# A token MLP's first product in layer one: ten of fourteen weight tiles taken as five pairs by seven half products, with two smaller edits elsewhere

## The chip, the cores and the metric

The kernel runs on one core of one Trainium2 chip. The metric is the device time of one execution in microseconds (us), as the median of three runs. A core has a matrix engine (TensorE, PE in the profile, with its weight loads as PEld), VectorE (DVE), ScalarE (ACT), GpSimd (POOL) and SyncE (SP), which issues the DMA transfers. Each engine works through its own list of instructions in order and waits on semaphores for the others.

## The reference, cut to what matters

```python
# x: (1, 2048 tokens, 640 channels); F = 1728 hidden
def _A_ref(x, w_r, w_i):
    X = rfft2(x);  X = X * (w_r + 1j * w_i)
    return irfft2(X, s=(S, D))

def _B_ref(x, w1, b1, w2, b2):
    h = _layernorm(x)                          # over channels
    u = gelu(einsum("bsd,sf->bdf", h, w1) + b1)  # over tokens
    return (einsum("bdf,fs->bds", u, w2) + b2).transpose(0, 2, 1)

x = x + _A_ref(_layernorm(x), A_w_r, A_w_i)    # layer 1, spectral
x = x + _B_ref(_layernorm(x), B_w1, B_b1, B_w2, B_b2)   # layer 1, MLP
x = x + _A_ref(_layernorm(x), A_w_r, A_w_i)    # layer 2, spectral
x = x + _B_ref(_layernorm(x), B_w1, B_b1, B_w2, B_b2)   # layer 2, MLP
```

## The kernel before, in words

All four stages run as matrix products on TensorE. Each factor of a product is split into a high and a low half-precision part, and a product is three matmuls (`mm3`): high weights by high input, high by low, low by high. One matmul has 128 x 128 weights and 320 columns; the 640 channels are two halves of 320 columns. The 2048 tokens are 16 token tiles (`NJ`), the 1728 hidden rows 14 hidden tiles (`NFT`), of which the last is half full. Nearly every instruction is recorded through the helper `call` at L58, so that in the profile the names of the tiles tell instructions apart, not lines.

**Layer one's MLP** is the function `b1st` (L1131). At its start there are 16 normalised token tiles `hf` (single precision) with their high parts `hh`. VectorE makes the low parts `hl` = `hf` - `hh`, 16 subtractions of 640 elements a row, in one go, while TensorE works on what needs only `hh`: `both_high` gives the high products of hidden tiles 0 and 1. Then the loop over the hidden tiles (L1212) runs: for tiles 0 and 1 the 32 matmuls each that need `hl` (`rest`, L1193), for tiles 2 to 12 all 96 matmuls (`both`: 16 token tiles by two halves by three), for tile 13 64. Tile 2's weights can be split only when its scale is known: TensorE sums the squares that ScalarE scanned, VectorE makes the scale from it in a chain of six small instructions (`scale1`, L291; `qt`, `qi`, `s`, `c` in the trace), ScalarE rounds the raw weights to the high part `wh`, VectorE makes the low part `wl`. After each hidden tile ScalarE and VectorE form its gelu (L1250 to L1256) into `uf`. `scale_u` and `usplit` (L1181) split that into `uh` and `ul`, on VectorE. The second product (L1290) takes the 14 hidden tiles in order as inputs for the 16 token tiles, adds the result to x and prepares the next spectral stage; after the last token tile a short chain, `a0_tail` (L603), prepares the last input while TensorE runs `warm` matmuls whose result isn't used.

**Layer two's MLP** (`b2nd`, L1366) already takes its second product in pairs of tiles by seven half products.

The work in these stages stands in the order of the code (`pin` is true) or is left to the framework's scheduler (`pin` is false). The spectral stages are ordered by a planner (`Plan`) from costs and due times in `add(...)` calls.

## Time and profile before

| | |
|---|---|
| median of three runs | 1010.33 us (1010.2 to 1010.74) |
| profiled execution, whole time | 1010.17 us |
| profiled execution, span of the trace | 1008.4 us |
| mean granted TensorE clock | 0.997 |
| busy: TensorE / VectorE / ScalarE / GpSimd | 976.7 / 710.3 / 592.2 / 251.6 us |
| first stage ends, layer one's spectral stage goes on | about 50 us |
| layer one's MLP starts / tile 2 starts / second product starts / ends | 168.2 / 195.7 / 349.0 / 542.7 us |

A row of the profile's timeline gives the start, the time taken by the whole group, the engine, the operation, what it writes `<-` what it reads, the sizes and, behind an x, how many instructions it groups; in brackets the idle time before it and what ended it. The view of windows gives each engine's busy time in a stretch of the span and in brackets the instructions; PEclk is the granted clock of TensorE as a share of the full one.

### The profile page before, as it was taken

What the parts mean: (1) busy time and instruction counts of PE and PEld (TensorE: products, weight loads), DVE (VectorE), ACT (ScalarE), POOL (GpSimd) and SP (SyncE); (2) the same over time, 40 slices, a digit from 0 to 9 for tenths busy, and PEclk for the clock granted to TensorE, in tenths of its full rate; (3) what the DMA queues carried; (4) which work ended last, traced back from release to release, by engine and by line L of the source; (5) the groups of instructions that cost most, each with busy time, mean ns of one, the idle gap of its engine ahead of it and who ended that gap; (6) DMA issues with size and microseconds to landing.
All of it is one profiled execution on the core that took longest, in us unless ns stands there. A gap on an engine that the chain in (4) does not pass through costs nothing. (4 is left out here: it accounts for less than half of the span.)

```text
span 1008.4 us, 22169 instructions
## 1 busy us (share of the span) xinstructions
PE 976.7 (97%) x8981; PEld 718.1 (71%) x8981; DVE 710.3 (70%) x1382; ACT 592.2 (59%) x926; POOL 251.6 (25%) x409
## 2 busy tenths in 40 slices
PE   5899999999999999999998999999999999999998
PEld 4678666777777777777777886667777777777776
DVE  7989678743336777777765896886644755988885
ACT  6978699564444565555542777964644545444531
POOL 7759786000000011111121796840000000000000
PEclk8999999999999999999999999999999999999999
DMA  8774275532222453443325532846222322545411
GB/s 318 252 220 111 80 226 159 163 94 76 84 85 73 141 192 133 140 138 126 106 83 174 161 117 77 236 151 209 85 84 85 95 88 80 163 152 188 145 45 53
DMA packets 53862, 135.75 MB, mean 135 GB/s; under 512 B 6376, under 2 KB 11392, under 8 KB 53760
## 3 DMA queue, kind: packets, MB, share of 16 engines
q1 hardware_dynamic: 53760, 134.35, 41.1%
q8 instruction: 70, 1.15, 0.5%
q14 instruction: 32, 0.26, 0.1%
HBM read 111.25 MB, written 23.07 MB: 133 GB/s over the span
## 5 line engine op out<-in xcount | busy, mean ns | idle before, releaser
L58 PEld LDWEIGHTS <-wh 128*128 128x128 f16 x2992 | 289.9, 98 | 114.1 <-issue 3.3
L58 PEld LDWEIGHTS <-wl 128*128 128x128 f16 x1616 | 158.0, 98 | 61.6
L58 PE MATMUL ps<-hh,wh 128*128 128x320 f16 x896 | 186.5, 299 | 1.6 <-ACT hh L58 1.6
L58 PE MATMUL ps<-hl,wh 128*128 128x320 f16 x896 | 184.7, 299 | 0.0
L58 PE MATMUL ps<-hh,wl 128*128 128x320 f16 x832 | 171.4, 299 | 0.0
L58 DVE SCALAR_TENSOR_TENSOR wl<-raw,s,wh 128x1024 f16<-128x1024 f32 (+2 forms) x88 | 110.5, 1273 | 46.8 <-ACT wh L58 46.7
L58 ACT ACTIVATE wh<-raw,s 128x1024 f16<-128x1024 f32 (+2 forms) x92 | 94.7, 1049 | 65.5 <-PE ps L58 58.9
L58 PE MATMUL ps<-uh,wl 128*128 128x320 f16 x448 | 133.1, 299 | 0.0
L58 PE MATMUL ps<-ul,wh 128*128 128x320 f16 x448 | 133.0, 299 | 0.0
L58 PE MATMUL ps<-uh,wh 128*128 128x320 f16 x416 | 124.3, 299 | 0.0
L58 ACT ACTIVATE junk<-raw 128x896 bf16<-128x896 f32 (+1 forms) x60 | 59.7, 995 | 44.1 <-DMA raw<-w 43.5
L58 PE MATMUL ps<-u,wo 128*128 128x320 f16 x504 | 69.9, 299 | 0.0
L58 DVE TENSOR_TENSOR xt<-xt,ps 128x320 f32<-128x320 f32 (+1 forms) x96 | 45.0, 490 | 30.6 <-ACT ec L58 20.3
L58 POOL TENSOR_TENSOR r<-v,mh 128x1 f32<-128x1 f32 (+1 forms) x56 | 33.6, 600 | 125.6 <-DVE nm L58 112.6
L58 PEld LDWEIGHTS <-wo 128*128 128x128 f16 x504 | 49.3, 98 | 19.1
L58 DVE BATCH_NORM_STATS2 st<-xt 128x6 f32<-128x320 f32 x128 | 56.2, 480 | 3.3 <-DMA xt<-x 2.7
L58 PE MATMUL ps<-tDi,yh 128*128 128x322 f16 x240 | 50.2, 299 | 0.0
L58 DVE TENSOR_SCALAR qt<-ps 128x1 f32<-128x1 f32 x14 | 2.1, 156 | 67.4 <-PE ps L58 67.4
L58 PE MATMUL ps<-u,wh 128*128 128x320 f16 x336 | 48.4, 299 | 0.0
L58 PE MATMUL ps<-u,wl 128*128 128x320 f16 x336 | 48.2, 299 | 0.0
L58 POOL MEMSET uh<- 64x640 f16 x1 | 0.8, 776 | 184.1 <-DVE ul L58 184.1
L58 PE MATMUL ps<-tm,F 128*128 128x128 f32 (+1 forms) x256 | 30.5, 317 | 15.0 <-ACT tm L58 11.5
(177 smaller groups left out, 1879.5 us busy)
## 6 DMA issues: line engine op xcount, KB each, us to landing
raw<-w SPq DMA_DIRECT2D x56, 512.0 KB, 3.6
xt<-x SPq DMA_DIRECT2D x80, 320.0 KB, 3.9
x<-xt SPq DMA_DIRECT2D x48, 320.0 KB, 2.5
raw<-w SPq DMA_DIRECT2D x32, 448.0 KB, 3.3
raw<-w2z SPq DMA_DIRECT2D x32, 448.0 KB, 3.4
w<-w SPq DMA_DIRECT2D x44, 321.0 KB, 3.6
out<-xt SPq DMA_DIRECT2D x15, 320.0 KB
stk<-rest SPq DMA_DIRECT2D x36, 64.0 KB, 2.7
```

Of the source, the lines that this page charges most:

```text
L58: i = f(*a, **k)
```

## The change

**Layer one's first product.** Hidden tiles 0, 1, 2 and 13 are computed as before (`plain`). Tiles 3 to 12 become five pairs (3, 4) to (11, 12). For each pair the weights form a 2 x 2 block matrix (two hidden tiles by two halves of the token tiles), the inputs another (two halves of the token tiles by the two column halves), and the four blocks of the result come from seven products of sums of blocks (Winograd's form of Strassen's method): `PQ` lists them. One of the seven is 8 token tiles by 3 matmuls of 320 columns, 24 matmuls; a pair has 168, where two tiles had 192. With it come:

- the input sums T1 to T4: `tsum(k)`, four subtractions of 320 elements a row on GpSimd for each of k = 0 to 7, and `tsplit(k)`, which splits them (1280 elements a row) into a high part on ScalarE and a low part on VectorE, in the memory of `hf`;
- the weight sums S1 to S4: `form`, four GpSimd instructions of 1024 elements a row a pair; the high part of each product's weights on ScalarE (`hi`) and the low part on VectorE (`lo`);
- `evict`, which adds the products into the results, on VectorE, ScalarE and, twice a pair, on GpSimd;
- `uh` made on ScalarE; for tiles 7 to 10 (`PT`) `ul` on GpSimd after a GpSimd multiplication (`MUL`); the last splits of `u` after the last product (`after`);
- the second product takes its inputs in the order 0, 1, 2, 13, 3 to 10, 12, 11 (`FO`).

**The first stage**: a third input tile is loaded ahead of the constants, one dummy ScalarE instruction stands at the start (`first`), one sum of the first tile goes from VectorE to GpSimd, the last two tiles are handled singly, one power is taken earlier.

**Between the layers** (`a0_tail`): the odd subtraction is done on GpSimd on the input without its mean removed (`a0_head`), as soon as the second half is there; the even addition takes away twice the mean in the same instruction; `z` is gone; the two additions and subtractions over 512 columns stand ahead of those over 128; `warm` has 52 matmuls for 64. In the second spectral stage two fetches wait for other events (`stack`, `w`).

The core of the diff:

```diff
+M0, PD = 3, 5
-            if o.pin:
+            if o.pin and (o.pin != "rest" or self is not o.PE):
...
-            add(("total", i), *(("G", .85) if i else ("V", .55)), [("diff", i)], e - 3.6, total, i, None if i else V)
+            v = i in ()
+            add(("total", i), *(("V", .55) if v else ("G", .85)), [("diff", i)], e - 3.6, total, i, V if v else None)
...
-        self.warm(room[:, 1], 64)
+        self.warm(room[:, 1], 52)
-        V.tensor_scalar(z[:, :D], xt, mv[:, 0:1], None, op0=ALU.subtract)
-        V.tensor_tensor(v2(eo, 1, 161), za, zb, op=ALU.add)
-        V.tensor_tensor(v2(eo, 322, 161), za, zb, op=ALU.subtract)
+        V.scalar_tensor_tensor(v2(eo, 1, 161), za, m2, zb, op0=ALU.subtract, op1=ALU.add)
...
+        TSPLIT = {(0, 6): 2, (0, 12): 3, (2, 1): 4, (2, 12): 5, (2, 14): 6, (NFT - 1, 4): 7}
+        def tsum(k):
+            fs = X[k % 5].rearrange("p a b c -> p (a b) c")
+            (b11, b12), (b21, b22) = ([self.hf[i][:, c] for c in range(2)] for i in (k, k + 8))
+            for o, x, y in ((0, b12, b11), (1, b22, fs[:, 0]), (2, b22, b12), (3, b21, fs[:, 1])):
+                G.tensor_tensor(fs[:, o], x, y, op=ALU.subtract)
+        def tsplit(k, hi=True, lo=True):
+            fs = X[k % 5].rearrange("p a b c -> p (a b) c")
+            if hi:
+                T.activation(four[k], fs, AF.Copy)
+            if lo:
+                V.tensor_tensor(four[k + 8], fs, four[k], op=ALU.subtract)
+        PQ = ("A11", "B11"), ("S1", "T1"), ("S2", "T2"), ("S3", "T3"), ("A12", "B21"), ("S4", "B22"), ("A22", "T4")
+        ops = [(d, *PQ[i]) for d in range(PD) for i in (range(7) if d < PD - 1 else (1, 2, 3, 6, 0, 4, 5))]
+        def form(n):
+            ...
+            G.tensor_tensor(o, x, y, op=op)
+        def hi(n):
+            ...
+            T.activation(wo[n][:, 0], src[n], AF.Identity, scale=s2[:, ops[n][0]:][:, :1])
+        def lo(n):
+            ...
+            V.scalar_tensor_tensor(
+                w[:, 1], src[n], s2[:, ops[n][0]:][:, :1], w[:, 0], op0=ALU.mult, op1=ALU.subtract
+            )
+        def product(n):
+            w = wo[n]
+            for j in range(8):
+                self.mm3(place(n), (w[:, 0, j], w[:, 1, j]), operand(ops[n][2], j), j == 0, j == 7)
...
         w = self.w.pop(0), self.w.pop(1)
+        pss = [self.big(), self.big()]
         self.both_high(pss, w, prod)
-        for ft in range(NFT):
+        self.pin = "rest"
+        for k in range(5):
+            tsum(k)
+        for k in range(2):
+            tsplit(k)
+            tsum(k + 5)
+            self.scan1(3 + k)
+        form(0)
+        for ft in (0, 1, 2, NFT - 1):
+            plain(ft)
+        self.pin = True
+        pairs()
+        after()
```

TensorE's list has 120 matmuls fewer in the pairs (five pairs by 24) and 12 fewer `warm` matmuls.

**Where instructions stand.** On GpSimd at the start of layer one's MLP, before (`r` is the root of the variance of the last token tile, `uh13` belongs to the end of the first product, `r_648` to the second product):

```order
L58 TENSOR_TENSOR r_486_3343<-v_483_3336,mh_63 128x1
L58 TENSOR_TENSOR nb_487_3345<-nm_484_3338,r_486_3343 128x1
L58 TENSOR_TENSOR r_491_3354<-v_489_3350,mh_63 128x1
L58 MEMSET uh13_499_3445 64x640
L58 TENSOR_TENSOR r_648_5407<-v_646_5403,mh_63 128x1
```

and now, from the same root on (`uf0` and `uf1` are where the input sums of k = 0 and 1 stand, `hf0`, `hf8` and so on the token tiles; 24 more rows of this kind, for the other k, follow, and then the weight sums `S`):

```order
L59 TENSOR_TENSOR r_491_3359<-v_489_3355,mh_63 128x1
L59 TENSOR_TENSOR uf0_500_3439<-hf0_295_2540 128x320
L59 TENSOR_TENSOR uf0_500_3439<-hf8_295_2548,uf0_500_3439 128x320
L59 TENSOR_TENSOR uf0_500_3439<-hf8_295_2548,hf0_295_2540 128x320
L59 TENSOR_TENSOR uf0_500_3439<-hf8_295_2548,uf0_500_3439 128x320
...
L59 TENSOR_TENSOR uf2_500_3441<-hf15_295_2555,uf2_500_3441 128x320
L59 TENSOR_TENSOR S_531_3889<-raw_504_3455,raw_505_3457 128x1024
L59 TENSOR_TENSOR S_534_3927<-S_531_3889,raw_502_3451 128x1024
```

Between the root and the end of the first product, where GpSimd had one MEMSET, there are now 32 sums of 320 elements and, behind them, the pairs' weight sums. Five sets of buffers hold the sums, so that the twenty instructions for k = 0 to 4 wait for no split, while those for k = 5 wait until `tsplit(0)` has read its set.

On VectorE, from the last low parts `hl` to the first gelu, before (`qt` to `c0` make the scale of hidden tile 2, `q` belongs to the gelu of tile 0, `wl` is tile 2's low weights):

```order
L58 TENSOR_TENSOR hl15_496_3420<-hf15_295_2550,hh15_493_3379 128x640
L58 TENSOR_SCALAR qt_76<-ps506_3488 128x1
L58 TENSOR_SCALAR qi1_508_3653<-qt_76 128x1
L58 TENSOR_SCALAR s0_72<-qi1_508_3653 128x1
...
L58 SCALAR_TENSOR_TENSOR q_510_3660<-q_510_3660,t_509_3659 128x640
L58 SCALAR_TENSOR_TENSOR wl_512_3667<-raw_494_3383,s0_72,wh_511_3666 128x1024
```

and now (`hf8`, `hf9` and `hf10` on the left are the low parts of the input sums of k = 0, 1 and 2, written where those token tiles stood):

```order
L59 TENSOR_TENSOR hl15_496_3425<-hf15_295_2555,hh15_493_3384 128x640
L59 TENSOR_TENSOR hf8_295_2548<-uf0_500_3439,hf0_295_2540 128x1280
L59 TENSOR_TENSOR hf9_295_2549<-uf1_500_3440,hf1_295_2541 128x1280
L59 TENSOR_TENSOR hf10_295_2550<-uf2_500_3441,hf2_295_2542 128x1280
L59 TENSOR_SCALAR qt_78<-ps508_3465 128x1
L59 TENSOR_SCALAR qi1_512_3675<-qt_78 128x1
...
L59 SCALAR_TENSOR_TENSOR q_514_3682<-q_514_3682,t_513_3681 128x640
L59 SCALAR_TENSOR_TENSOR wl_516_3687<-raw_494_3388,s0_74,wh_515_3686 128x1024
```

Three subtractions of 1280 elements now stand between the last `hl` and the chain that gives tile 2 its scale. On TensorE the order up to tile 2 is what it was.

On GpSimd in the pairs (`raw` is raw weights, as are `wh_541` and `wl_542`, whose memory holds raw weights there; `uf0` holds the pair's results):

```order
L59 TENSOR_TENSOR S_546_4043<-raw_503_3453,S_534_3927 128x1024
L59 TENSOR_TENSOR uf0_500_3439<-uf0_500_3439 128x320
L59 TENSOR_TENSOR S_552_4111<-wh_541_4008,wl_542_4010 128x1024
L59 TENSOR_TENSOR uf0_500_3439<-uf0_500_3439 128x320
L59 TENSOR_TENSOR S_561_4192<-S_552_4111,raw_517_3692 128x1024
L59 TENSOR_TENSOR S_568_4232<-raw_517_3692,wh_541_4008 128x1024
L59 TENSOR_TENSOR S_576_4304<-raw_518_3694,S_561_4192 128x1024
```

Each pair now has four sums of 1024 elements and two of 320 on GpSimd, where before it had nothing.

More of the change, by code (lines that the diff above doesn't have):

```diff
@@ L203, in setup @@
         nc.vector.memset(self.eps, EPS)
+        self.first = base.tile([128, 1], F32, name="first")
+        nc.scalar.activation(self.first, self.eps, AF.Identity)
         self.b1 = base.tile([128, NFT], F32, name="b1s")
@@ new lines, in b1st, with pair, raw @@
+        src, wo, bank = {}, {}, {}
+        s2, c2 = (self.base.tile([128, PD], F32, name=f"{a}1") for a in ("s2", "c2"))
+        def pair(d):
+            a, b = (slice(M0 + 2 * d + i, M0 + 2 * d + i + 1) for i in range(2))
+            V.tensor_tensor(s2[:, d:d + 1], self.st[0][:, a], self.st[0][:, b], op=ALU.min)
+            V.tensor_tensor(c2[:, d:d + 1], self.ct[0][:, a], self.ct[0][:, b], op=ALU.max)
+        def raw(d, a):
+            return self.wraws[M0 + 2 * d + int(a[1]) - 1][int(a[2]) - 1]
@@ new lines, in split, with after @@
+        def split(i, hi=False, lo=False):
+            for k in HI[i] if hi else ():
+                usplit(k, uf[k], lo=False)
+            for k in LO[i] if lo else ():
+                usplit(k, uf[k], hi=False)
+        def after():
+            p1, (q,) = done
+            split(7, lo=True)
+            for e in p1:
+                gelu1b(*e)
+            split(7, hi=True)
+            gelu0b(*q[1:])
+            gelu1a(*q)
+            split(8, hi=True)
+            split(8, lo=True)
+            gelu1b(*q)
+            split(9, hi=True)
+            self.wopen(NFT + 1)
+            self.wsplit(NFT + 1, lo=False)
+            split(9, lo=True)
+            self.wsplit(NFT + 1, hi=False)
@@ L1299, in b1st @@
             pss = ps, self.big() if last else ps
-            order = [(ft, a) for ft in range(NFT) for a in range(2)]
+            order = [(ft, a) for ft in FO for a in range(2)]
             if last:
```

331 lines of the change are left out of this document (264 added, 67 removed).

## Prediction

> **What bounds the kernel now.** I read the page first (busy times and the slices), then the windows around layer one's MLP, then the timelines of its first thirty microseconds engine by engine, then the first stage, as the place where GpSimd (POOL) and VectorE (DVE) work side by side today. From the page, the busy times and two rows of its 40 slices:
>
> ```profile
> PE 976.7 (97%) x8981; PEld 718.1 (71%) x8981; DVE 710.3 (70%) x1382; ACT 592.2 (59%) x926; POOL 251.6 (25%) x409
> PE   5899999999999999999998999999999999999998
> POOL 7759786000000011111121796840000000000000
> ```
>
> TensorE (PE) is busy all the time but at the start; GpSimd stands at 0 through layer one's first product. The windows give busy time of PE, PEld, DVE, ACT and POOL, each with its count, then the clock:
>
> ```profile
> 160.00:180.00 20.00, 19.20 (x126) 12.88 (x126) 17.39 (x51) 17.12 (x26) 8.69 (x17) 1.00 0.53 165
> 180.00:200.00 20.00, 19.62 (x148) 14.04 (x147) 13.79 (x28) 10.74 (x18) 0.00 (x0) 1.00 0.44 144
> 200.00:220.00 20.00, 20.00 (x153) 14.43 (x151) 9.20 (x20) 13.46 (x20) 0.00 (x0) 1.00 0.37 116
> ```
>
> From 200 on TensorE never waits and VectorE has half its time free; before 190 VectorE, at 17.39 of 20, has nothing to give. TensorE's timeline there, and below it VectorE's and GpSimd's:
>
> ```profile
> 182.54 4.51 PE L58 MATMUL ps<-hh,wl 128*128 128x320 f16 x32
> 186.89 4.51 PE L58 MATMUL ps<-hl,wh 128*128 128x320 f16 x32
> 191.29 4.51 PE L58 MATMUL ps<-hl,wh 128*128 128x320 f16 x32
> 195.66 0.43 PE L58 MATMUL ps<-hh,wh 128*128 128x320 f16 x2
> ```
>
> ```profile
> 173.60 2.47 DVE L58 SCALAR_TENSOR_TENSOR wl<-raw,s,wh 128x1024 f16<-128x1024 f32 x2
> 175.99 11.85 DVE L58 TENSOR_TENSOR hl<-hf,hh 128x640 f16<-128x640 f32 x16
> 191.50 0.16 DVE L58 TENSOR_SCALAR qt<-ps 128x1 f32<-128x1 f32 x1 [3.67 <-PE ps L58]
> ...
> 172.94 0.55 POOL L58 TENSOR_TENSOR r<-v,mh 128x1 f32<-128x1 f32 x1 [0.54 <-ACT hh L58]
> ```
>
> The last `hl` is done at 175.99 + 11.85 = 187.84. TensorE takes the first at 186.89 and two matmuls, 0.27 us, for each, so the last is wanted at 191.0: the cover is 10 us for the first `hl` (done at 176.7) and 3.1 us for the last. VectorE then waits 3.67 us for TensorE, and the weights of tile 2 are there the moment TensorE wants them (195.66).
>
> **The change part by part.**
>
> *Fewer matmuls.* 32 matmuls run from 182.54 to 186.89, 4.35 us, 0.136 us each. Five pairs save 5 x 24 = 120: 120 x 0.136 = -16.3 us, as TensorE's list says and as long as TensorE stays the bound.
>
> *The input sums.* `tsum` puts 32 GpSimd subtractions of 320 elements behind the root at 172.94, twenty of them free of any split. They start at 173.5, beside VectorE's two `wl` and sixteen `hl`. What GpSimd and VectorE do to each other shows in two places of the trace, first in the first stage, then in the spectral stage (the last row is the same small GpSimd operation undisturbed):
>
> ```profile
> 39.67 2.19 DVE L58 TENSOR_TENSOR F<-zz 128x640 f32<-128x640 f32 x2
> ...
> 40.13 2.46 POOL L58 TENSOR_TENSOR zz<-zz 128x320 f32<-128x320 f32 x2
> ...
> 132.86 0.73 DVE L58 SCALAR_TENSOR_TENSOR wl<-raw,s,wh 128x512 f16<-128x512 f32 x1
> ...
> 133.19 0.45 POOL L58 TENSOR_TENSOR nb<-nm,r 128x1 f32<-128x1 f32 x1
> ...
> 172.21 0.19 POOL L58 TENSOR_TENSOR nb<-nm,r 128x1 f32<-128x1 f32 x1
> ```
>
> An `nb` of 0.19 us takes 0.45 and ends 0.05 us after the `wl` beside it; two folds of 640 and two sums of 320 take 42.59 - 39.67 = 2.92 us together, 1.46 us for one of each. So the two engines take turns whole instruction by whole instruction, 0.74 for VectorE's and about 0.7 for GpSimd's. With turns: two `wl` (1.23 each) and two sums end at 173.6 + 2 x 1.93 = 177.5; sixteen `hl` by 1.46 less the last sum end at 177.5 + 23.4 - 0.7 = 200.2 instead of 187.84, +12.4 us. That is more than the cover above: from about the ninth `hl` on TensorE waits for each one, the first `rest` ends at 200.6, the second at 205.0 (4.35 later) instead of 195.6.
>
> No row shows `hl` itself beside a GpSimd sum, only two other VectorE operations with two inputs; held to those alone the sum would have +1.5 here (the first rival). The Trainium skill, "SBUF — State Buffer", section "Who interferes with whom", says that a VectorE instruction with two SBUF inputs excludes a GpSimd instruction that reads SBUF, for its whole length; that covers `hl`, would give the +12.4, and speaks against this change. The rows agree with it.
>
> *The three splits.* Between the last `hl` and `qt` VectorE now makes three low parts of 1280 elements. By `hl` (11.85 / 16 = 0.74 for 640) one takes 1.4 to 1.5 us, and GpSimd's next sum takes its turn in between: 3 x (1.45 + 0.7) = 6.4, so `qt` comes at 206.6 (before 191.50, +15.1). From `qt` to tile 2's first matmul were 195.66 - 191.50 = 4.2 us; there one gelu step and two `wl` now meet sums for two turns, 5.5 us: tile 2 starts at 212.1, +16.4 us. TensorE idles from 205.0 to 212.1. ScalarE's copies of 1280 and the scans lie in its idle time (10.74 busy of 20). In SP's queue the raw weights of tile 13 now come with those of 3 and 4; those of tile 5 wait for tile 2's split, near 210, and are wanted one pair after tiles 3 and 4, some 40 us later: nothing.
>
> *The clock after that.* TensorE's first long wait today:
>
> ```profile
> 16.65 5.26 PE L58 MATMUL ps<-tm,F 128*128 128x128 f32 x32 [2.00 <-ACT tm L58]
> 22.67 3.01 PE L58 MATMUL ps<-tm,F 128*128 128x128 f32 x32
> ...
> 15.00:20.00 5.00, 3.35 (x19) 2.74 (x20) 4.42 (x12) 4.68 (x11) 5.00 (x7) 0.60 1.05 399
> ```
>
> After 2.0 us of waiting the granted clock is 0.60 over five microseconds, and 32 matmuls take 5.26 us for the later 3.01: +2.2 us, which I add once. The Trainium skill, "TensorE: Matmul & The Clock Gate", Part 1, gives the time at half rate after idling as about 3.4 us, which would cost 1.7 as an estimate from that page; the row decides. The sums and splits for k = 5 to 7 wait for the earlier splits, and the products that use T1 to T4 wait for them: by a turn or two at a time 0.5 to 3.8 us, I take 1.4. The lead-in together: 16.4 + 2.2 + 1.4 = +20 us, from 14 (no clock loss, cheaper splits, one turn in five missed) to 24.
>
> *The pairs.* Work for a pair, by these groups (count, busy, mean in ns):
>
> ```profile
> L58 POOL TENSOR_TENSOR yl<-Y,yh 128x512 f16<-128x512 f32 x30 | 34.8, 1160 | 5.9 <-ACT yh L58 4.6 <-issue 1.3
> L58 POOL TENSOR_TENSOR zz<-zz 128x320 f32<-128x320 f32 x31 | 31.2, 1024 | 6.4 <-ACT zz L58 6.3
> L58 DVE SCALAR_TENSOR_TENSOR wl<-raw,s,wh 128x1024 f16<-128x1024 f32 x48 | 61.4, 1283 | 46.7 <-ACT wh L58 46.7
> L58 DVE SCALAR_TENSOR_TENSOR xt<-ps,cp,xt 128x320 f32<-128x320 f32 x32 | 17.6, 550 | 20.7 <-ACT m L58 11.7 <-PE ps L58 8.9
> L58 ACT ACTIVATE wh<-raw,s 128x1024 f16<-128x1024 f32 x48 | 54.7, 1142 | 58.2 <-PE ps L58 53.0 <-issue 5.2
> 193.39 0.82 DVE L58 SCALAR_TENSOR_TENSOR q<-q,t 128x640 f32<-128x640 f32 x1 [0.79 <-ACT q L58]
> ```
>
> TensorE needs 168 x 0.136 = 22.8 us for a pair. GpSimd's sums of 1024 show nowhere; by 1160 ns for 512 they are at most 2.3 us each, by the per-element rate of the sums of 320 (0.7) 2.2, less a fixed part I take 1.95. The two engines' turns then add up: seven low parts at 1.23, four gelu steps at 0.75, four sums of 1024 at 1.95 and two of 320 at 0.75 are 8.6 + 3.0 + 7.8 + 1.5 = 20.9 us of 22.8. The additions from PSUM (0.55, six a pair) have one SBUF input; I count them outside. So it fits with 8% to spare, and a late sum delays a product now and then: +2 us over five pairs, from 0 to +8.
>
> *The end of the pairs.* After the last product, tile 11 goes through two ScalarE steps of 0.8, a gelu step of 0.82, a tanh, another step, `uh` and `ul`, about 6.5 us; the order `FO` needs it thirteenth, after 13 x 6 x 0.136 = 10.6 us. On VectorE five `ul` at 0.82 stand around it, and tile 4's, needed after 4.1 us, stands behind a gelu step that waits for ScalarE. +2 us, from 0 to +4.
>
> *Between the layers*, the rows of before:
>
> ```profile
> 542.52 3.74 PE L58 MATMUL ps<-ones 128*128 128x128 bf16 x64
> 544.15 0.54 DVE L58 TENSOR_SCALAR z<-xt,mv 128x640 f32<-128x640 f32 x1
> 544.80 0.89 DVE L58 TENSOR_TENSOR eo<-z 128x320 f32<-128x320 f32 x2
> 545.80 1.03 DVE L58 TENSOR_TENSOR f<-eo 128x256 f32<-128x256 f32 x4
> 547.46 0.28 PE L58 MATMUL ps<-tM,fh 128*128 128x128 f16 x2 [1.20 <-ACT fh L58]
> ```
>
> `z` (0.54) and one `eo` (0.45) leave VectorE's chain, a scalar `m2` and a small `eo` (0.15 each) come in: -0.7; `fh` waits for two `f` instead of four: -0.3. GpSimd's subtraction lies under the statistics, and `warm` at 52 x 0.058 = 3.0 us ends as much earlier as the chain. -1.0 us, from -1.3 to -0.7; what is late next is `fl`, behind `fh` as before.
>
> *The first stage.*
>
> ```profile
> 20.00:40.00 20.00, 17.34 (x167) 12.86 (x165) 19.73 (x41) 18.89 (x43) 20.00 (x26) 0.93 0.77 246
> 45.51 3.02 PE L58 MATMUL ps<-tm,F 128*128 128x128 f32 x32 [0.33 <-ACT tm L58]
> ```
>
> GpSimd is full there, so the sum that moves to it costs one turn (+0.85); at the end half of the last 3.02 us of matmuls is done earlier (-1.5), and the earlier dummy instruction spares some tenths at the start. I take -0.5, from -2 to +1. The two fetches in the second spectral stage lie under a busy TensorE: nothing, and without that cover a fetch's few tenths.
>
> *The sum.* Against the profiled execution's own 1010.17 (its span is 1008.4, the rest lies around it; the median of three runs, 1010.33, is 0.16 more): 1010.17 - 16.3 + 20 + 2 + 2 - 1.0 - 0.5 = 1016.4. With all bounds low 1010.17 - 16.3 + 14 + 0 + 0 - 1.3 - 2 = 1004.6, high 1030; they will not all fall together, so this case's own range is 1009 to 1023.
>
> **The rivals.**
>
> *VectorE is not held up* (or GpSimd waits for it): then the `hl` end near 188 as now, the splits (3 x 1.45 = 4.35) take VectorE's 3.67 us of waiting and delay `qt` by about 0.7 to 1.5, and the gain stays: 1010.17 - 16.3 + 1.5 + 1 + 1 - 1.5 = 996. If GpSimd only gets every second turn, half the delay stays, 1005. For it: nothing shows `hl` itself beside GpSimd, and TensorE is busy throughout. Against it: `nb` and the folds above. Together 0.34.
>
> *It cancels*: the lead-in costs 14 and the rest nothing, within 2 us of now. 0.08.
>
> *The pairs bind too*: if GpSimd's sums take 2.3 and the PSUM additions (6 x 0.55) take turns as well, a pair needs 20.9 + 1.4 + 3.3 = 25.6 for 22.8, five pairs +14 instead of +2: 1028. It decides from 22.8 us a pair; against it speaks that one of the two inputs there is PSUM. 0.10.
>
> That the change doesn't do what it says is ruled out by TensorE's list.
>
> **How the numbers follow.** The forecast has 0.48, the case of equal time 0.08, the faster ones 0.34, the one with bound pairs 0.10. About 0.2%, 2 us, is what a measurement of this kernel can tell from no change: faster 0.34, same 0.08, slower 0.58. The predicted time is the forecast's, 1016.4. The range leaves out the faster rival's better half (0.17) and little above: 1000 to 1024.
>
> **What would show it.** Right: the `hl` group 23 to 25 us long instead of 11.85 with GpSimd's sums between, waits of TensorE for VectorE's `hl` from 189 to 201, `qt` near 206, tile 2 near 212, the granted clock below 1 for some microseconds after, and the pairs without waits. Wrong: `hl` done before 190, and tile 2 before 198; or a second product that starts before 345 (349.0 less 16.3 plus 20 is 353 by the forecast). The gain itself is wrong if a pair takes more than 23 us.

## The result, and the profile after

The changed kernel takes 1036.78 us (median of six runs, 1035.26 to 1037.89), the kernel before in the same rounds 1010.39 us (1010.2 to 1010.94): a ratio of 1.0259, with an interval of 1.0248 to 1.027. It is slower, as forecast, but by 26 us where 6 were forecast, and 1036.78 lies above the range, which ended at 1024.

The busy times, the two rows of the 40 slices and the span, of the changed kernel's page:

```profile
span 1033.3 us, 22106 instructions
PE 973.3 (94%) x8849; PEld 709.6 (69%) x8849; DVE 793.0 (77%) x1424; ACT 629.9 (61%) x975; POOL 393.2 (38%) x482
PE   5899999788999888999999899999999999999998
POOL 7759687973666621111112397860000000000000
```

TensorE's list is 132 shorter (120 in the pairs, 12 `warm`), as the forecast had it, yet its row has dips at 7 and 8 where it read 9; GpSimd has 6s and 7s where it stood at 0. Every matmul is in both traces, so starts can be counted off. Where the 25 us of the profiled executions (1035.26 against 1010.17) come from, in us from the span's start:

| place | before | after | difference | forecast |
|---|---|---|---|---|
| first stage, to its first spectral product | 50.65 | 51.81 | +1.2 | -0.5 |
| MLP of layer one starts | 168.19 | 169.36 | (the same 1.2) | |
| lead-in: from there to the first product of the pairs (before: to the end of the 160 matmuls of two hidden tiles, a full and a half one, 21.7 us behind 195.66) | 49.2 | 68.9 | +19.8 | +20 |
| ten hidden tiles, now five pairs | 131.65 | 126.07 | -5.6 | -16.3 + 2 |
| second product, to the first `warm` matmul (with the join at the end of the pairs) | 193.5 | 203.2 | +9.7 | +2 |
| from there to layer two's MLP | 122.97 | 122.86 | -0.1 | -1.0 |

The lead-in is as forecast in its sum and in its shape. VectorE, GpSimd and TensorE there, from their timelines:

```profile
178.44 22.53 DVE L59 TENSOR_TENSOR hl<-hf,hh 128x640 f16<-128x640 f32 x16
200.89 6.28 DVE L59 TENSOR_TENSOR hf<-uf,hf 128x1280 f16<-128x1280 f32 x3
207.09 0.14 DVE L59 TENSOR_SCALAR qt<-ps 128x1 f32<-128x1 f32 x1
```

```profile
174.64 0.86 POOL L59 TENSOR_TENSOR uf<-hf 128x320 f32<-128x320 f32 x1
179.21 1.44 POOL L59 TENSOR_TENSOR uf<-hf,uf 128x320 f32<-128x320 f32 x1
```

```profile
192.61 0.43 PE L59 MATMUL ps<-hl,wh 128*128 128x320 f16 x2 [0.97 <-DVE hl L59]
...
210.02 0.45 PE L59 MATMUL ps<-hh,wh 128*128 128x320 f16 x2 [1.85 <-ACT wh L59]
227.74 0.45 PE L59 MATMUL ps<-hh,wh 128*128 128x320 f16 x2 [1.19 <-DVE wh L59]
238.29 0.31 PE L59 MATMUL ps<-hh,wo 128*128 128x320 f16 x1 [1.69 <-ACT wo L59]
```

Sixteen `hl` take 22.53 us (11.85 before, 22.7 by the forecast's working); a GpSimd sum takes 0.86 us alone and 1.44 beside an `hl`, which is one turn of each engine, sixteen times over. TensorE gets two matmuls of work for every 1.4 us. The last `hl` ends at 200.97 (forecast 200.2), `qt` comes at 207.09 (206.6), tile 2 at 210.02 (212.1). The windows (columns as in the prediction) show the clock lower there, and what the start of the second product looks like:

```profile
190.00:200.00 10.00, 4.82 (x22) 2.22 (x21) 10.00 (x8) 5.39 (x7) 9.84 (x8) 0.77 0.00 0
200.00:210.00 10.00, 7.46 (x42) 4.43 (x39) 9.04 (x11) 2.73 (x4) 9.92 (x8) 0.72 0.01 2
...
370.00:380.00 10.00, 6.60 (x47) 4.38 (x45) 9.74 (x9) 7.01 (x11) 3.43 (x2) 1.00 0.66 226
```

From 190 to 200 VectorE is busy for all ten microseconds with only eight instructions. TensorE does not stand still there, it gets small portions; the clock is down to 0.77 and 0.72 all the same. Cut finer, the windows have it at 0.50 from 195.43 to 205.67 and 1.00 on both sides.

In the pairs the forecast fails. What GpSimd does between the first product and the end of the pairs, by operation and shape (busy us, mean ns of one | idle before), and a stretch of GpSimd's and VectorE's timelines:

```profile
L59 POOL TENSOR_TENSOR uf<-uf 128x320 f32<-128x320 f32 x9 | 16.1, 1791 | 30.8 <-DVE uf L59 30.7
...
L59 POOL TENSOR_TENSOR uf<-uf,su 128x640 f32<-128x640 f32 x4 | 7.9, 1982 | 3.2 <-DVE uf L59 3.2
L59 POOL TENSOR_TENSOR S<-raw,wh 128x1024 f32<-128x1024 f32 x2 | 6.7, 3340 | 0.0
L59 POOL TENSOR_TENSOR S<-wh,wl 128x1024 f32<-128x1024 f32 x2 | 4.7, 2351 | 0.0
```

```profile
310.64 3.34 POOL L59 TENSOR_TENSOR S<-raw,wh 128x1024 f32<-128x1024 f32 x1
313.94 2.95 POOL L59 TENSOR_TENSOR S<-raw,S 128x1024 f32<-128x1024 f32 x1
```

```profile
311.68 2.98 DVE L59 SCALAR_TENSOR_TENSOR q<-q,t 128x640 f32<-128x640 f32 x1
314.58 0.54 DVE L59 SCALAR_TENSOR_TENSOR uf<-ps,c,uf 128x320 f32<-128x320 f32 x1
315.05 2.92 DVE L59 SCALAR_TENSOR_TENSOR wo<-S,s,wo 128x1024 f16<-128x1024 f32 x1
```

A weight sum takes 2.35 us where VectorE leaves it alone (the last group; VectorE was on small instructions then) and 3.0 to 3.3 elsewhere; the sum of 320, 0.86 alone, takes 1.79 and not 0.75, because it too has to wait for its turn. On the other side a gelu step `q` of 0.82 takes 2.98, since it stands behind a whole weight sum, and a low part of 1.28 takes 2.92. The addition from PSUM between them, which has one input in SBUF, keeps its 0.54 us beside the second sum: it takes no turn. TensorE's waits in the pairs, in sum (us, times, longest), and the two longest for VectorE's weights from its timeline:

```profile
PE ps L59 <- DVE wo L59: 5.3, 5, 2.3
PE ps L59 <- ACT junk L59: 2.9, 5, 1.0
...
350.13 3.16 PE L59 MATMUL ps<-hf,wo 128*128 128x320 f16 x22 [2.31 <-DVE wo L59]
354.79 0.45 PE L59 MATMUL ps<-hh,wo 128*128 128x320 f16 x2 [1.23 <-DVE wo L59]
```

From pair to pair it is 27.1, 23.45, 23.45, 25.3 and 26.75 us, where 168 matmuls by 0.136 need 22.85. Together that is 126.07 - 114.2 = 11.9 us over; the ten tiles before were 131.65 - 130.56 = 1.1 over their 960 by 0.136, so 10.8 of it are new. `junk` is ScalarE's scan of the next weights: 2.9 us of the waits are for ScalarE, which the forecast of the pairs didn't price.

In the second product, which had no wait for inputs before, TensorE's list of waits from 364 to 560 reads:

```profile
PE ps L59 <- DVE hf L59: 5.0, 4, 1.6
PE ps L59 <- ACT fh L59: 2.1, 2, 1.8
PE ps L59 <- DVE fl L59: 1.2, 2, 0.6
```

`hf` are here the low parts `ul` of the last pairs, standing in the memory of `hf`; `fh` (made by ScalarE) and `fl` (by VectorE) are the parts of the next layer's input.

### The profile page after: what moved, and what is told of

Its sections match the earlier page's. It is cut to its first block, busy times and chain, and to the rows that moved or that the text cites. A ratio compares the mean times of both kernels' runs of the same rounds, so it can differ in the third digit from the quotient of the medians.

```text
span 1033.3 us, 22106 instructions
## 1 busy us (share of the span) xinstructions
PE 973.3 (94%) x8849; PEld 709.6 (69%) x8849; DVE 793.0 (77%) x1424; ACT 629.9 (61%) x975; POOL 393.2 (38%) x482
## 3 DMA queue, kind: packets, MB, share of 16 engines
q8 instruction: 69, 1.13, 0.5%
## 5 line engine op out<-in xcount | busy, mean ns | idle before, releaser
L59 PEld LDWEIGHTS <-wh 128*128 128x128 f16 x2352 | 229.4, 98 | 104.2 <-issue 11.7
L59 PE MATMUL ps<-hf,wh 128*128 128x320 f16 x864 | 179.6, 299 | 5.0 <-DVE hf L59 5.0
L59 PEld LDWEIGHTS <-wo 128*128 128x128 f16 x1344 | 131.3, 98 | 63.4 <-DVE wo L59 7.0
L59 PE MATMUL ps<-hf,wl 128*128 128x320 f16 x448 | 133.1, 299 | 0.0
L59 PE MATMUL ps<-hl,wh 128*128 128x320 f16 x576 | 120.4, 307 | 5.9 <-DVE hl L59 5.7
L59 PE MATMUL ps<-hh,wh 128*128 128x320 f16 x576 | 117.6, 300 | 5.3 <-ACT hh L59 2.3
L59 DVE SCALAR_TENSOR_TENSOR wl<-raw,s,wh 128x896 f16<-128x896 f32 (+2 forms) x68 | 84.2, 1261 | 45.2 <-ACT wh L59 45.2
L59 PE MATMUL ps<-hh,wl 128*128 128x320 f16 x512 | 102.5, 300 | 1.3 <-DVE wl L59 1.3
L59 ACT ACTIVATE wh<-raw,s 128x896 f16<-128x896 f32 (+2 forms) x70 | 70.4, 1031 | 50.9 <-PE ps L59 38.8
L59 PE MATMUL ps<-hf,wo 128*128 128x320 f16 x480 | 67.2, 299 | 3.2 <-DVE wo L59 3.2
```

Of the source, the lines that this page charges most:

```text
L59: i = f(*a, **k)
```

## Experiments

Where no ratio is given, a kernel ran once; the six runs of the change lie between 1035.26 and 1037.89 us.

**The lead-in: is it GpSimd's reading?** My theory was that the sums cost what they do because GpSimd reads SBUF beside VectorE's instructions with two inputs; the rival, that the sums, splits and weights are simply late whatever GpSimd reads. First, the sums as instructions that only write (the products of the pairs then have constants for their input sums):

```diff
-                G.tensor_tensor(fs[:, o], x, y, op=ALU.subtract)
+                G.memset(fs[:, o], 0.01)
```

> The changed kernel (1036.8 us) with the 32 input sums of tsum replaced by GpSimd memsets of the same memory; T1 to T4 are left out, so the products that use them work on a constant. GpSimd then writes in the same places of its list and reads nothing; the lists of the other engines are the same row for row. Theory (turns between GpSimd's reads and VectorE's two-input instructions): the sixteen hl take about 12 us instead of 22.5 and end near 189.5, qt comes near 195 instead of 207.1, tile 2 starts near 199 instead of 210.0, the granted clock stays at 1 in 190 to 240, the first product of the pairs starts near 221 instead of 238.3, and the whole takes 1016 to 1020 us. Rival (the order of the work: three splits, scans and a longer ScalarE list stand ahead of tile 2's scale): hl is no shorter than 20 us or tile 2 still starts after 207, and the whole stays above 1030 us.

Measured: 1022.44 us, some 14 less than the changed kernel and 2.4 above the range.

```profile
177.60 11.85 DVE L59 TENSOR_TENSOR hl<-hf,hh 128x640 f16<-128x640 f32 x16
...
175.04 6.20 POOL L59 MEMSET uf<- 128x320 f32 x20
...
223.64 0.31 PE L59 MATMUL ps<-hh,wo 128*128 128x320 f16 x1 [1.02 <-ACT wo L59]
```

The `hl` are back at 11.85 us, though GpSimd writes beside the first of them; tile 2 comes 11.8 us earlier, the first product of the pairs 14.65 of the 19.8. The pairs still take 126.3, and the first of them 27.11 as in the change. Then the reverse: the kernel before with twenty sums whose result nobody uses, placed where the change has its first twenty.

```diff
+        self.pin = True
+        for k in range(5):
+            for c in range(4):
+                G.tensor_tensor(uf[NFT - 1][:, c % 2], self.hh[k][:, c % 2], self.hh[k + 8][:, c % 2], op=ALU.subtract)
+        self.pin = False
```

> The kernel before, with nothing of the change but twenty GpSimd subtractions of 320 elements put where the changed kernel has its first twenty input sums; they read the high parts of token tiles and nothing uses their result. TensorE's, VectorE's and ScalarE's lists are those of before row for row. Theory (turns): the sixteen hl take 22 to 26 us instead of 11.85, tile 2 starts near 206 instead of 195.7, and the whole becomes 1019 to 1023 us though nothing waits for these sums. Rival (GpSimd's sums as such cost nothing; the delay comes from the splits and waits that hang on them): 1010 to 1011 us.

Measured: 1019.25 us against 1010.74, ratio 1.0091 (1.0074 to 1.0108).

```profile
177.52 21.36 DVE L58 TENSOR_TENSOR hl<-hf,hh 128x640 f16<-128x640 f32 x16
...
173.25 26.28 POOL L58 TENSOR_TENSOR uf<-hh,hh 128x320 f32<-128x320 f16 x20
...
192.29 0.43 PE L58 MATMUL ps<-hl,wh 128*128 128x320 f16 x2 [0.90 <-DVE hl L58]
```

The sums alone, with no one waiting for them, cost 8.5 us: 21.36 us for the `hl`, and the same waits in TensorE. The two runs together show the cause; the forecast's first rival, that VectorE isn't held up, is refuted by them. The Trainium skill, "SBUF — State Buffer", section "Who interferes with whom", says that a VectorE instruction with two SBUF inputs contends with a GpSimd instruction that reads SBUF and not with one that only writes it; 22.53 against 11.85 us agrees with both halves.

**Can the lead-in be put in another order?** All three kernels do the full computation. First, the low parts of the first three input sums, and the sums of k = 5 to 7, behind tile 2's weights:

```diff
-                    tsplit(k, lo=k != 3)
+                    tsplit(k, lo=ft > 0)
...
+                for k in range(3):
+                    tsplit(k, hi=False)
+                    tsum(k + 5)
...
-            tsplit(k)
-            tsum(k + 5)
+            tsplit(k, lo=False)
```

> The changed kernel with the low parts of the input sums of k = 0, 1 and 2 and the sums of k = 5, 6 and 7 moved behind the split of tile 2's weights; the computation is the same. It parts the delay by the sixteen hl from that by the three splits. Expected by turns: hl as slow as now (22.5 us), but qt near 202 instead of 207.1 and tile 2 near 206 instead of 210.0; the later sums arrive some 4 us later and may hold up the second product of the first pair; the whole 1031 to 1035 us. Rival (the wait only moves: what the splits delay comes back at the first pair): within 1.5 us of 1036.8.

Measured: 1036.16 us, ratio 1.025 (1.0233 to 1.0267), the same as the changed kernel. `qt` came at 201.91 and tile 2 at 208.06, only 2 us earlier, and tile 13 then waited:

```profile
225.48 0.44 PE L59 MATMUL ps<-hh,wh 128*128 128x320 f16 x2 [4.17 <-DVE wh L59]
238.57 0.31 PE L59 MATMUL ps<-hh,wo 128*128 128x320 f16 x1 [2.55 <-ACT wo L59]
```

The first product stands at 238.57 for 238.29: the wait had moved, as the rival said. Second, the sums held back until the last `hl` is done, by a copy on GpSimd that reads it, and the rest as in the last kernel:

```diff
+        gate = self.t(p, [128, 1], F16, "gate", 1)
+        G.tensor_copy(gate, self.h[NJ - 1][1][:, 0, :1])
```

> As e4_scale_first, and GpSimd waits for the last hl before its first input sum (one small copy that reads it); the computation is the same. The sums then run from 190 to about 215 beside tile 2 and not beside the hl. Theory (turns): hl 12 us long, tile 2 near 198 instead of 208, the first product of the pairs near 221 instead of 238.6, some waits for late sums in the first pair, the whole 1020 to 1026 us. Rival (the sums can't be had without their cost, a later start only moves the waits to the first pair): the second pair starts no earlier than 262 (now 265.7), the whole 1032 or more.

Measured: 1038.75 us, ratio 1.0277 (1.0262 to 1.0293); missed. The `hl` took 11.84 us, but ScalarE's copies of the sums stand ahead of its gelu steps in its own list, and they now waited for GpSimd, and VectorE for them:

```profile
206.31 1.18 DVE L59 SCALAR_TENSOR_TENSOR q<-q,t 128x640 f32<-128x640 f32 x1 [11.96 <-ACT q L59]
```

Third, those copies too behind tile 2's weights, and the later ones spread over tiles 2 and 13, with the same copy in front:

```diff
-        TSPLIT = {(0, 6): 2, (0, 12): 3, (2, 1): 4, (2, 12): 5, (2, 14): 6, (NFT - 1, 4): 7}
+        TSPLIT = {(2, 1): 2, (2, 5): 3, (2, 11): 4, (2, 15): 5, (NFT - 1, 4): 6, (NFT - 1, 10): 7}
...
+                for k in range(2):
+                    tsplit(k)
+                    tsum(k + 5)
...
-            tsplit(k)
-            tsum(k + 5)
```

> As e12_sums_after_hl, where ScalarE waited 12 us for the sums because its copies of them stood ahead of tile 2's weights; now those copies too come behind tile 2's weights, two there and the other six in tiles 2 and 13. The computation is the same. Theory (turns and list order are the whole lead-in): hl 12 us, tile 2 near 199, the pairs' first product near 223 and the second near 228, the whole 1019 to 1026 us. Rival (as e12: a later start moves the waits to the first pair): second product of the first pair after 238, the whole 1030 or more.

Measured: 1034.43 us, ratio 1.0233 (1.0219 to 1.0247); missed by 8 us. Tile 2 starts at 197.03, better than expected, but:

```profile
217.71 0.71 PE L59 MATMUL ps<-hh,wh 128*128 128x320 f16 x2 [6.74 <-DVE wh L59]
235.64 0.71 PE L59 MATMUL ps<-hf,wo 128*128 128x320 f16 x2 [3.87 <-ACT wo L59]
...
231.25 0.85 POOL L59 TENSOR_TENSOR uf<-hf,uf 128x320 f32<-128x320 f32 x1
```

The sums now last until 232.1 and meet VectorE's weights and gelus instead of its `hl`. Of the 13.0 us that tile 2 gains (197.03 for 210.02), the second pair keeps 2.9 (262.48 for 265.40). In the whole time this order keeps some 2.4 us; the rest of the turns is paid elsewhere ahead of the second pair.

**The pairs: GpSimd too slow, or the turns?** The weight sums as instructions that only write (constants in the place of S1 to S4); then the same three in a row, so that GpSimd is busy as long as a real sum is undisturbed (0.95 + 0.95 + 0.42 = 2.32 us for 2.35); then the sums on VectorE:

```diff
-            G.tensor_tensor(o, x, y, op=op)
+            G.memset(o, 0.01)
```

> The changed kernel with the 20 weight sums of form replaced by GpSimd memsets of 1024 elements; S1 to S4 are left out. The input sums are as in the changed kernel. Theory (turns): the start of the pairs stays near 238, the five pairs take 117 to 121 us instead of 126.1 (840 matmuls at 0.136 would be 114.2), as VectorE's low parts of weights no longer wait; the whole takes 1029 to 1033 us. Rival (the pairs are late because ScalarE's and VectorE's own steps and scans are, whatever GpSimd does): the pairs still take 125 us or more and the whole stays within 1.5 us of 1036.8.

```diff
-            G.tensor_tensor(o, x, y, op=op)
+            for q in (o, o, o[:, :3]):
+                G.memset(q, 0.01)
```

> As e2_forms_memset, but each weight sum is replaced by three memsets that together last about as long as an undisturbed sum (2.35 us), so that GpSimd is as busy and its results come as late as with real sums, while it reads nothing. Theory (turns with VectorE): within 2 us of e2_forms_memset (1023.8). Rival (GpSimd is simply late with the sums, since 2.35 us each is more than was allowed for): 1031 us or more.

```diff
-            G.tensor_tensor(o, x, y, op=op)
+            V.tensor_tensor(o, x, y, op=op)
```

> The changed kernel with the 20 weight sums computed by VectorE instead of GpSimd; the computation is the same. They cost VectorE about 1.2 us each, 4.8 us a pair, where turns cost it up to 2.35 each. Theory (turns): the pairs take 118 to 122 us instead of 126.1 and the whole 1028 to 1032 us. Rival (VectorE has no room for them): the pairs stay at 125 us or more, and the whole at 1035 or more.

Measured: 1023.8, 1024.81 and 1031.32 us. The first gains 13 us, more than I expected, 9.1 of them in the pairs (25.3, 22.9, 22.9, 23.0 and 22.9 us) and 2.9 ahead of them; TensorE's waits in the pairs fall to 1.1 us for VectorE's weights and 0.6 for ScalarE's scans. The group that stands for the sum in the second:

```profile
L59 POOL MEMSET S<- 128x1024 f32 x40 | 38.1, 952 | 12.2 <-DVE wo L59 7.8 <-DVE wh L59 3.2
L59 POOL MEMSET S<- 128x384 f32 x20 | 8.4, 418 | 1.1
```

With GpSimd busy for as long as the real sums would be undisturbed, the pairs take 117.7 us for 117.0: what costs is the turns, not GpSimd's own length. On VectorE the sum takes less, 1.39 us for 3.0 to 3.3, and the whole is 5.5 us better than the change; but the pairs take 124.7 and not the 118 to 122 that I expected, since TensorE waits 4.1 us for VectorE's weights in the last one, which takes 29.2.

All of GpSimd's reads in the MLP out at once (input sums, weight sums, `ul`, the multiplication, and the additions of `evict` are constants):

```diff
-                G.tensor_tensor(x[:, 0, 1], x[:, 1, 0], x[:, 1, 1], op=ALU.add)
+                G.memset(x[:, 0, 1], 0.01)
...
-                    G.tensor_tensor(ul[ft], t, uh[ft], op=ALU.subtract)
+                    G.memset(ul[ft], 0.01)
```

> The changed kernel with every GpSimd instruction that its first product added (input sums, weight sums, the additions of products, the multiplication and the low parts for tiles 7 to 10) replaced by a memset of what it wrote; these sums are left out, the lists of TensorE, VectorE and ScalarE are the same row for row. Theory (turns): the lead-in as in e1_sums_memset, the pairs 114 to 117 us instead of 126.1, TensorE's waits at the start of the second product under 2 us instead of 5.7, and the whole 1000 to 1006 us. Rival (the new work itself is too long for VectorE and ScalarE in these places): the whole stays above 1020 us.

Measured: 1006.26 us, 30.5 less than the change: 14.3 as with the input sums alone, 13.0 as with the weight sums alone, and 3.2 that are left for the rest if the parts add up. So even with nothing read on GpSimd, and part of the work not done at all, 4.6 of the 16.3 us remain as a gain. In this run the lead-in still costs 2.4 us (first product at 220.99, nominally 217.36 + 1.2), the pairs lose 1.4 (the first takes 23.86) and the second product 8.7. Of these 8.7, half the clock from 364.71 to 368.12 can be 1.7 at most; TensorE waits 2.2 us for low parts, where I expected under 2, and 2.7 for `fh`. So most of the second product's delay is there without any of GpSimd's reads.

**The second product.** Each of these kernels has a piece of the suspected backlog moved or taken out. VectorE does the low parts of the last pairs, the weights, the scale and the preparation of the next layer at once; ScalarE scans the next weights ahead of `fh`. First, `fh` ahead of the scans in all token tiles, then another order of the low parts, then both:

```diff
-                if i == 6 and j < 2:
-                    self.scan1(m + 2)
                 if i == 10:
+                    if j:
+                        f = self.a0_lo(*self.a0_hi(f))
+                    if j < 2:
+                        self.scan1(m + 2)
                     self.scan1(m + 3 if j else NFT + NJ)
                     plus_b(j)
-                    if j:
-                        f = self.a0_lo(*self.a0_hi(f))
```

> The changed kernel with one edit in the second product: ScalarE makes fh, the high part for the next stage's first transform, ahead of the weight scans of that token tile and not behind them (four scans of 1.1 us in the first tiles); the computation is the same. Theory (list order on ScalarE): TensorE's wait of 2.15 us for fh at the first transform falls to under 0.8, that of 0.6 at the second goes, and the second product (203.2 us now, 193.5 before) takes 200.5 to 202. Rival (fh is late because VectorE's f is): the waits stay within 0.5 us.

```diff
-        LO = (), (), (), (), (), pick(0, 1), pick(8, 2, 3), pick(4, 9), pick(5, 6, 10, 7, 11), pick(12, 13)
+        LO = (), (), (), (), (), pick(0, 1), pick(8, 2, 3), pick(4, 5, 6, 9), pick(10, 7, 11), pick(12, 13)
```

> The changed kernel with two low parts of u (tiles 4 and 5) ahead of the gelu step of tile 11 in VectorE's list, which waits for ScalarE; the computation is the same, and on VectorE two instructions change places with one. Theory (list order on VectorE): the first two waits of TensorE in the second product, 1.91 and 1.77 us, fall to under 0.6 together, the later two may grow as tile 11 comes later, and the second product takes 200 to 202 us. Rival (VectorE is behind by the work itself, turns included): the sum of the four waits, 5.7 us, changes by less than 1.5.

> The changed kernel with both edits of e14 and e15. If list order on ScalarE and VectorE makes the second product's delay, its 9.7 us fall to 5 or 6 and the whole to 1031 to 1034 us; if not, the whole stays within 1.5 us of 1036.8.

Measured: 1045.33, 1036.11 and 1044.44 us (the last with a ratio of 1.0336, 1.0319 to 1.0353). The first order makes it worse, and neither expectation for the third held: the first wait for `fh` falls from 1.85 to 0.21 (the expectations count from start to start, hence 2.15), but the scans now stand behind it and ahead of `s1h` in every token tile, VectorE waits for that (2.49 us in the tile at 437.62), and a new wait of TensorE appears in nearly all:

```profile
PE ps L59 <- DVE fl L59: 6.8, 12, 0.6
```

The second order cuts the waits for low parts to two, of 3.3 us for 5.0, but a wait for a scan (0.9 us) comes in, and the second product takes 209.6 us to the next layer's first product (209.23 in the change, 200.95 before). In this run the clock is at 0.50 from 394.29 to 397.71, which the change has nowhere in this stage; that can hide up to 1.7 us of a gain, so the run doesn't show that the order is worth nothing.

```profile
PE ps L59 <- DVE hf L59: 3.3, 2, 1.7
PE ps L59 <- ACT junk L59: 0.9, 1, 0.9
```

Then four low parts out of it (constants in their place), and, in another kernel, two scans in the second token tile (the sums of squares are constants):

```diff
-            if lo:
+            if lo and 3 <= ft <= 6:
+                G.memset(ul[ft], 0.01)
+            elif lo:
```

> The changed kernel with the low parts of u for tiles 3 to 6 left out on VectorE (GpSimd sets them to a constant); nothing else in the lists of TensorE, VectorE and ScalarE moves. Theory (VectorE still has 3.3 us and more of the pairs' work to do when the second product starts): TensorE's four first waits, 5.7 us more than its pace, fall to under 1.5, and the second product takes 203 to 206 us from its first matmul to the next stage's first, where it takes 209.2 now. Rival (the waits have another cause, such as ScalarE's high parts): 208 or more.

```diff
-                    self.scan1(m + 2)
+                    if j:
+                        self.ssq[m + 2] = self.t(self.base, [128, 2], BF16, "sq", 3)
+                        G.memset(self.ssq[m + 2], 1.0)
+                    else:
+                        self.scan1(m + 2)
```

> The changed kernel with the two extra weight scans at the second token tile of the second product left out (their sums are set to a constant); nothing else moves. Theory (fh waits behind ScalarE's four scans): TensorE's wait for fh, 2.15 us, falls to under 0.8 as fh comes 2.1 us earlier, and the second product takes 207 to 208 us from its first matmul to the next stage's first instead of 209.2. Rival (fh is held by VectorE's f): within 0.5 us of 209.2.

Measured: 1036.04 and 1033.76 us. The first is inconclusive: the constants stood in GpSimd's own queue and came late there, so that one wait was exchanged for another, and the clock is at 0.50 for two stretches of 3.41 us in the second product, where the change has 1.00.

```profile
PE ps L59 <- POOL hf L59: 3.0, 2, 2.1
```

The second held: to the next layer's first product it takes 207.24 us, 2.0 less than in the change, as expected. The rows of `fh` on ScalarE, of the change and of this kernel:

```profile
390.76 0.95 ACT L59 ACTIVATE junk<-raw 128x896 bf16<-128x896 f32 x1
...
392.43 0.72 ACT L59 ACTIVATE fh<-f 128x640 f16<-128x640 f32 x1
```

```profile
390.84 0.74 ACT L59 ACTIVATE fh<-f 128x640 f16<-128x640 f32 x1 [0.40 <-DVE f L59]
```

One token tile's scans ahead of `fh` are thus 2.0 of the 9.7 us.

**The small edits, each put into the kernel before.** Theory: the shorter chain between the layers gives 1.0 us and the first stage costs 1.2; rival for the first: the clock or a transfer takes it back. The chain with 52 `warm` matmuls and with 64, and the first stage alone (the diffs are those of the change, in `a0_tail` with its `a0_head`, and in the first stage's plan):

```diff
-        self.warm(room[:, 1], 64)
+        self.warm(room[:, 1], 52)
...
-        V.tensor_scalar(z[:, :D], xt, mv[:, 0:1], None, op0=ALU.subtract)
...
+        V.scalar_tensor_tensor(v2(eo, 1, 161), za, m2, zb, op0=ALU.subtract, op1=ALU.add)
```

> The kernel before with the change's a0_tail and a0_head alone (52 warm matmuls); the computation is the same. In the changed kernel the chain between the layers was 1.4 us shorter, but TensorE then ran at half clock for some microseconds and the stage behind came 1.3 us later. Theory (with 12 warm matmuls fewer the clock drops before the chain is through): 1010.0 to 1010.6 us, the gain eaten. Rival (the clock drop came from something else in the changed kernel): 1008.8 to 1009.3 us.

> As t52_before_tail, but with 64 warm matmuls as before. Theory (the warm matmuls set the clock): no half clock at the start of layer two's spectral stage, the first product there 1.4 us earlier, 1008.8 to 1009.3 us in all, which would be faster than both kernels. Rival (the clock depends on when the chain ends, not on 12 matmuls): as t52_before_tail within 0.3 us.

> The kernel before with the change's edits to the first stage alone (third load ahead, dummy ScalarE instruction, the first tile's sum on GpSimd, last two tiles singly, one power earlier); the computation is the same. In the changed kernel layer one's spectral stage began 1.2 us later. Theory (the stage is bound by GpSimd, which has one sum more): the spectral stage's first product at 51.8 instead of 50.65 and 1011.3 to 1012.0 us in all. Rival (the delay came from elsewhere, the edits gain as I forecast): 1009.5 to 1010.2 us.

Measured: ratios 1.0000 (0.9991 to 1.0008), 0.9995 (0.9986 to 1.0004) and 1.0016 (1.0006 to 1.0025). The chain is 0.75 us shorter in both of the first two, and with 52 matmuls it is all given back, not by the clock, which the windows have at 1.00, but by a transfer that TensorE then waits for, with 0.5 us in the kernel before:

```profile
PE ps L58 <- DMA stk<-rest: 1.7, 1, 1.7
```

My theory of the clock fell there for the kernel before. In the changed kernel no such wait is in the list; there the next stage's first spectral product comes 1.44 us earlier behind the start of `warm` (6.00 for 7.44), 1.33 of that is gone again by layer two's MLP, and in between the clock is down:

```profile
575.00:580.00 5.00, 5.00 (x55) 5.00 (x54) 0.83 (x1) 1.38 (x2) 0.00 (x0) 0.73 0.95 313
```

On balance the clock takes no more than 0.4 us of it: the kernels with the first and with both orders above have the same list there and a clock of 1.00, need 122.48 and 122.46 us for 122.86, and wait 0.7 us for `stk` again.

The first stage's edits alone give its whole +1.2: the first spectral product at 51.85 for 50.65 (51.81 in the change). GpSimd, full there as the prediction's window shows, has one sum more and now waits 1.13 us for ScalarE ahead of a late one; which of these edits costs the 1.2 no run shows.

No version that does the full computation beats the kernel before by more than the measurement can tell.

## Why the prediction was right or wrong

- **Fewer matmuls**: right, 120 by 0.136 us; pairs two and three take 23.45 us, 0.6 above the 22.85 they were given.
- **The input sums**: right, in mechanism and size: turns instruction by instruction, +10.7 us on the `hl` group (forecast +10.9 to its own working) and TensorE waiting from the tenth `hl` on (it runs 18 matmuls, nine `hl`, before the first wait), for the ninth forecast.
- **The three splits**: right, 6.28 us for 6.4.
- **Tile 2, the clock, the sums for k = 5 to 7**: tile 2 came 13.2 us late in its own stage where 16.4 were forecast, because its first matmuls need only the high weights that ScalarE makes; the low ones, behind a gelu step of 1.24 us and with turns of their own (3.68 us for two), cost a wait of 1.33 a little later. The rest of the +19.8 came with further late operands, at tile 13 and the first product (waits of 1.19 and 1.69). The clock, down at 0.77, 0.72 and 0.83 between 190 and 220, was priced at +2.2, and that term isn't found: from 210 to 220 the change has 0.83 and the kernel with four low parts out, whose lists are the same there, has 1.00, and their lead-ins are 68.93 and 68.92 us. The operands are late either way; the slower matmuls only fill the waits. So the sum of +20 is right partly by luck: tile 2 was put 3.2 us too high, the clock's 2.2 isn't found, and the waits behind tile 2 made up for both.
- **The pairs**: the step that failed, with +2 (0 to +8) forecast. In the place of -16.3 the stage gave -5.6, so 10.7 were lost. Two terms were too small: the weight sum was taken at 1.95 us and is 2.35 undisturbed, and the sums of 320 at 0.75, which are 0.86 undisturbed and took 1.79 with the wait for their turn. More than that, the step added up a pair's work and compared the sum with 22.8 us. With 2.35 in the place of 1.95 the same sum is 22.5, which fits, and pairs two and three did nearly fit, with 0.6 over. The loss is in the other three: +4.3 in the first, +2.5 and +3.9 in the last two. That it hangs on the turns of the weight sums is shown: where they only write, the last two take 22.97 and 22.87 us, though GpSimd's multiplications (four times 1.98 us, not counted at all), the tile splits and the final scale are still there. In the first pair, 27.11 us, leaving out the reads of the input sums alone changes nothing (27.11), of the weight sums alone gives 25.30, of both 23.86. The clock isn't the cause there: it is 0.50 from 239.81 to 243.22 in the change and 1.00 in the kernel with two scans out, and both take 27.1. An average decided a question that each pair's worst stretch decides; that the last two are worse than the middle ones because more work comes together there is argued from the lists. The rival that made the pairs bind had the right direction and, with 2.3, the right sum; the additions from PSUM that it also counted kept their 0.54 us. The Trainium skill, "GPSIMD Engine Reference", section "3.1 Elementwise — side-by-side cycle accounting", gives 4.5 us for such a sum of 2048 single-precision elements, from which 2.2 for 1024 would be an estimate; the 2.35 measured agrees, and it was nearer than my 1.95.
- **The end of the pairs and the second product**: the place was named, the size was wrong (+2, at most +4, for +9.7). The forecast counted one tile's gelu and five low parts, and put at nothing that ScalarE scans the next weights ahead of `fh`; those scans are shown to be 2.0 of the 9.7. It did not count either that these low parts take turns with GpSimd (three of them in 4.76 us where 0.82 each is their length alone). But the turns are the smaller part: with all of GpSimd's reads out the second product still loses 8.7 us, or 7.0 if its stretch at half clock cost the full 1.7. What the rest is stays open. That VectorE, at 9.74 of 10 us busy, hands a backlog on to the next layer's preparation is argued from the windows; no run took the backlog away.

```profile
370.85 4.76 DVE L59 SCALAR_TENSOR_TENSOR hf<-uf,su,hf 128x640 f16<-128x640 f32 x3
```

- **Between the layers**: the chain is 0.75 us shorter for the 1.0 forecast. What the forecast named as late next, `fl`, is not what takes the gain back: it is the transfer of `stk` when the edit stands in the kernel before, and in the changed one a clock of 0.73, or that transfer again where the clock stays at 1.00.
- **The first stage**: wrong in sign, +1.2 for -0.5, outside the bounds (-2 to +1). The turn that GpSimd gets in addition was priced at 0.85; the gain of 1.5 set against it doesn't come, since the last root comes 1 us later (45.34 for 44.33).
- **The sum**: 8.7 (pairs) + 7.7 (second product) + 1.7 (first stage) + 0.9 (between the layers) - 0.2 (lead-in) is, but for rounding, the 18.9 by which the profiled 1035.26 stands above 1016.4.

## What to carry over

Before work is given to GpSimd beside VectorE instructions with two SBUF inputs, add both engines' times, as they are undisturbed, over the shortest stretch in which a result is due, not over the mean of the stage: here the average pair fitted and the first and last did not. Taking the sums' order apart moved the wait from tile 2 to tile 13 and on to the first pair; the best of three orders kept 2.4 us of a loss of 26, while leaving the sums' reads out gave 14 and 13. And small edits that shorten a chain are worth measuring one by one: two of them here gave nothing or cost something.

## What the runs showed of the hardware

- Where both have a full list, GpSimd instructions that read SBUF and VectorE instructions with two SBUF inputs alternate, one whole instruction each: one `hl` (0.74 us alone) and one sum of 320 (0.86 alone) together take 1.41 us, so that an engine with long instructions holds up the other's short ones (a `q` of 0.82 us took 2.98). Instructions that only write, on GpSimd, cost VectorE nothing (11.85 us for the `hl`), and an addition from PSUM takes no turn either (0.54).
- The granted clock falls without any long wait: with two matmuls for every 1.4 us, and no wait over 0.97, it fell at 195.43. The windows of the change have it at 0.50 from there for 10.24 us, and from 212.50, 239.81 and 574.31 for 3.41 us each: whole multiples of 3.41, as are the distances between these times.
- The same waits can bring it down or not. Around 370, with two waits of some 1.5 us, it stayed at 1.00 in the change and fell in the kernel with two scans out. What differs is where the stretches of 3.41 us lie. First the change, whose stretch holds one of the two waits, then the other kernel, whose stretch holds most of both:

```profile
369.51:372.92 3.41, 1.78 (x12) 1.03 (x11) 2.81 (x3) 3.41 (x6) 1.42 (x1) 1.00 0.07 24
```

```profile
368.33:371.75 3.42, 0.97 (x6) 0.58 (x6) 2.60 (x5) 3.16 (x5) 0.37 (x2) 1.00 0.46 162
371.75:375.16 3.41, 3.13 (x12) 1.63 (x12) 3.41 (x3) 1.71 (x3) 3.24 (x2) 0.50 0.55 140
```

TensorE is busy for 1.78 us of its stretch in the one and 0.97 in the other. In the change it was busy 0.88, 1.16 and 0.86 us in the stretches ahead of 195.43, 212.50 and 239.81. The border isn't sharp: 1.57 us were followed by the fall at 574.31, and 1.56 us, from 389.99 on, by none.

The Trainium skill, "TensorE: Matmul & The Clock Gate", Part 1, describes a window of about 3.4 us that runs on freely, so that the phase decides; the stretches of 3.41 us in these traces agree.
